# One weight load issued as two: wq by 16 and 112 partitions at the head of a decode step

## The chip, the cores and the metric

The kernel runs on one core of a Trainium2 chip. The metric is the device time of one execution in microseconds, the median of several runs. The kernel before takes 694.68 us (three runs, 694.67 to 694.69). Times inside an execution come from one profiled execution and count from the start of its span.

## What is computed

One decode step for one token of width 512. Two branches are mixed by a gate: attention with 32 query heads over 8 key/value heads and a cache of 32,768 positions, and a gated feed-forward layer of width 1,792. Everything is float32. Cut to what matters:

```python
# x (1,1,512); k_cache, v_cache (1,8,32768,128); wq (512,4096); wo (4096,512)
# w1, w3 (512,1792); w2 (1792,512); gate_w (512)
g = sigmoid((x * gate_w).sum(-1, keepdims=True))
q = (x @ wq).reshape(1, 1, 32, 128).transpose(0, 2, 1, 3)
k, v = repeat(k_cache, 4, axis=1), repeat(v_cache, 4, axis=1)
p = softmax(einsum("bhqd,bhkd->bhqk", q, k) * 128 ** -0.5)
a = einsum("bhqk,bhkd->bhqd", p, v).transpose(0, 2, 1, 3).reshape(1, 1, 4096) @ wo
b = (silu(x @ w1) * (x @ w3)) @ w2
return g * a + (1 - g) * b
```

Keys and values are 134 MB each; with the weights the kernel reads 296.23 MB from memory.

## The kernel before

The program is written out by hand: every engine has its list of instructions, and semaphores order them. Three buffers of 128 partitions by 64 KiB, `ra`, `rb` and `rc`, take all the large loads in turn. A load that fills one of them is 8 MiB, one contiguous row of 65,536 bytes for each partition.

SyncE issues all large loads (lines 115 to 149), so they form one queue. At its head stand five loads that wait for nothing: wq into all of `rc` (line 115), w1 and w3 into two parts of `rb` (116 and 117, rows of 28,672 bytes), and the first half of head 0's keys into `ra` in two parts (118 and 119). The next one, the second half of those keys into `rb` (line 121), waits until the feed-forward matmuls have read w1 and w3 from there. From then on, for each of the eight heads, two loads of keys go to `ra` and `rb` and two loads of values to `rc`, each issued when the buffer's last reader has signalled. The last head's values go to `ra` and `rb`, and wo and w2 close the queue. ScalarE issues two small loads, x and gate_w, of 2 KB each.

TensorE first turns x into columns and forms the gate's sum. Then it waits for wq (line 189) and multiplies x with it (line 194); after that it waits for w1 and w3 and does the same for the feed-forward layer (line 221). VectorE moves the query into place (206, 210), and GpSimd builds from it the windows of weights for the scores (249). Then comes a loop over heads. VectorE turns the keys in the buffer in blocks of 32 x 32 (line 335), TensorE takes the scores (line 262), the exponentials are taken on ScalarE, and one head later TensorE multiplies the probabilities with the values (line 276). At the end TensorE applies wo and w2 (lines 418 to 435).

A load's semaphore counts up by 16 when the load is complete. TensorE waits for wq with `pe.wait_ge(l_q, 16)`.

Of the kernel before, what the change touches and what calls it, by code (L numbers as in the profile page):

```python
# [9 lines left out]
P = 128  # L10
# [14 lines left out]
@with_exitstack  # L25
def kernel(ctx, tc, x, k_cache, v_cache, wq, wo, w1, w3, w2, gate_w, out):
    with tc.tile_critical():
        _program(tc.nc, x, k_cache, v_cache, wq, wo, w1, w3, w2, gate_w, out)


def _program(nc, x, k_cache, v_cache, wq, wo, w1, w3, w2, gate_w, out):
    pe, dve, act, pool, sp = nc.tensor, nc.vector, nc.scalar, nc.gpsimd, nc.sync
# [5 lines left out]
    NC = D // P  # L38
# [7 lines left out]
    def sb(name, *shape):  # L46
        return nc.alloc_sbuf_tensor(name, [P, *shape], F32).ap()

    def token(name):
        return nc.alloc_semaphore(name)  # L50
# [5 lines left out]
    ra, rb, rc = sb("ra", W), sb("rb", W), sb("rc", W)  # L56
# [34 lines left out]
    l_x, l_q, l_k0 = token("l_x"), token("l_q"), token("l_k0")  # L91
# [20 lines left out]
    kd = k_cache.rearrange("a h (p m n) d -> (a h) m p (n d)", p=P, m=2, n=NK)  # L112
    vd = v_cache.rearrange("a h (r p n) d -> (a h) r p (n d)", r=2, p=P, n=NK)
    half = W // 2
    sp.dma_start(rc, wq.rearrange("(p c) n -> p (c n)", c=NC)).then_inc(l_q, 16)
    sp.dma_start(rb[:, 0:NC * F], w1.rearrange("(p c) f -> p (c f)", c=NC)).then_inc(l_w1, 16)
    sp.dma_start(rb[:, NC * F:2 * NC * F], w3.rearrange("(p c) f -> p (c f)", c=NC)).then_inc(l_w3, 16)
    sp.dma_start(ra[:, 0:half], kd[0, 0][:, 0:half]).then_inc(l_k0, 16)
# [67 lines left out]
    dve.tensor_copy(xp[:, :, 0], mc[:, NC:2 * NC]).then_inc(t_x, 1)  # L186
    take(t_x, 2)
    n_gate = c_q.by(pe.matmul(mc[:, 0:1], ones[0:1], gsm[0:1], start=True, stop=True))
    pe.wait_ge(l_q, 16)
    for c in range(NC):  # L190
        for b in range(2):
            for j in range(4):
# [144 lines left out]
    def scaled(h):  # L337
        dve.wait_ge(c_h.sem, h + 1)
        return local.by(dve.scalar_tensor_tensor(  # L339
            otall[:, REP * h:REP * h + REP], mb[:, 0:REP], gate[:, 0:1], recip, op0=ALU.mult, op1=ALU.mult  # L340
        ))
# [57 lines left out]
    n = scaled(HKV - 1)  # L399
# [81 lines left out]
```

## Time and profile before

| what | value |
|---|---|
| median of the runs | 694.68 us |
| the profiled execution | 694.79 us |
| its span, first to last instruction | 692.5 us |
| mean granted TensorE clock | 0.783 |
| busy: TensorE, VectorE, ScalarE, GpSimd | 367.8, 309.3, 37.3, 7.1 us |
| moved from memory | 296.23 MB, 428 GB/s over the span |
| wq, from issue to landing | 21.8 us |

The profile shows one execution. In its table of slices, each digit is the busy share of a fortieth of the span in tenths. In rows of stages, the numbers are the stretch, its length, each engine's busy time with the number of its instructions, the granted clock, the mean busy share of the 16 DMA engines and what they moved in GB/s. A DMA packet is counted in the stretch in which it starts. In rows of the timeline, the numbers are start and length in microseconds, the engine (with a q for its queue, which issues loads) and line, what it writes and reads, and in brackets how long the engine idled before and what ended that.

### The profile page before, as it was taken

How to read it: one execution, taken by the hardware profiler on the slowest of the kernel's cores; microseconds unless marked ns; L12 is line 12 of the kernel's file. 1: busy time of each engine (PE TensorE's matmuls, PEld its weight loads, DVE VectorE, ACT ScalarE, POOL GpSimd, SP SyncE). 2: the span in 40 equal slices, each digit the busy share in tenths (PEclk: the TensorE clock that was granted, in tenths of full speed). 3: DMA queues.
4: the chain of work that ended last, by engine and by line, in shares of the span. 5: the costliest groups of instructions: out<-in, count | busy, mean ns of one | idle time of the engine just before them, and what ended most of it. 6: DMA issues, size and time to landing. Idle time of an engine off the chain costs nothing. (4 is left out here: it accounts for less than half of the span.)

```text
span 692.5 us, 6603 instructions
## 1 busy us (share of the span) xinstructions
PE 367.8 (53%) x2952; PEld 106.6 (15%) x2952; DVE 309.3 (45%) x208; ACT 37.3 (5%) x93; POOL 7.1 (1%) x41
## 2 busy tenths in 40 slices
PE   1626355456463734566463744466473835376475
PEld 1100011103010111103010121113010301113122
DVE  1129378191725447091816446181816356181000
ACT  0000011002000010002000010002000010001000
POOL 0000000000000000000000000000000000000000
PEclk9976598879677966778786966788677967768779
DMA  9999999999999999999999999999999999999996
GB/s 375 429 437 450 424 432 425 462 428 424 428 435 428 439 450 424 428 428 435 436 450 424 432 428 435 428 454 428 428 428 435 428 440 447 424 428 428 435 419 283
DMA packets 6069, 296.35 MB, mean 428 GB/s; under 512 B 678, under 2 KB 682, under 8 KB 940
## 3 DMA queue, kind: packets, MB, share of 16 engines
q1 hardware_dynamic: 6056, 296.23, 99.1%
q8 instruction: 6, 0.10, 0.1%
q14 instruction: 3, 0.02, 0.0%
q10 hardware_dynamic: 4, 0.00, 0.0%
HBM read 296.23 MB, written 0.00 MB: 428 GB/s over the span
## 5 line engine op out<-in xcount | busy, mean ns | idle before, releaser
L335 DVE STREAM_TRANSPOSE rb<-rb 128x2048 f32<-128x2048 f32 x64 | 141.8, 2275 | 150.9 <-DMA rb<-in_A_k_cache_dram 150.9
L335 DVE STREAM_TRANSPOSE ra<-ra 128x2048 f32<-128x2048 f32 x64 | 141.4, 2275 | 46.2 <-DMA ra<-in_A_k_cache_dram 46.2
L262 PE MATMUL psum<-rb,winbuf 128*32 128x512 f32 x512 | 91.9, 796 | 125.2 <-PEq L109 125.2
L276 PE MATMUL psum<-rc,prob 128*32 128x512 f32 x896 | 114.0, 666 | 42.7 <-PEq L109 42.7
L262 PE MATMUL psum<-ra,winbuf 128*32 128x512 f32 x512 | 82.8, 743 | 91.6 <-PEq L109 91.6
L276 PEld LDWEIGHTS psum<-rc,prob 128*32 128x32 f32 x896 | 33.7, 121 | 119.2 <-issue 119.2
L370 DVE TENSOR_REDUCE mx<-psum 128x4 f32<-128x1024 f32 x8 | 9.8, 1225 | 82.3 <-PE psum L286 82.3
L262 PEld LDWEIGHTS psum<-rb,winbuf 128*32 128x32 f32 x512 | 13.1, 120 | 201.9 <-issue 201.9
L262 PEld LDWEIGHTS psum<-ra,winbuf 128*32 128x32 f32 x512 | 14.6, 120 | 151.9 <-issue 151.9
L350 ACT COPY sbuf<-psum 128x512 f32<-128x512 f32 x16 | 9.8, 615 | 483.6 <-PE psum L262 483.6
L382 ACT ACTIVATE prob<-psum,nm 128x256 f32<-128x256 f32 x32 | 18.9, 695 | 36.5 <-DVE nm L379 36.5
L286 PE MATMUL psum<-ident,sbuf 128*64 128x64 f32 x512 | 16.7, 223 | 0.8 <-PEq L109 0.8
L286 PEld LDWEIGHTS psum<-ident,sbuf 128*64 128x64 f32 x512 | 15.6, 138 | 7.6 <-issue 7.6
L339 DVE SCALAR_TENSOR_TENSOR otall<-psum,gate,recip 128x4 f32<-128x4 f32 x8 | 1.7, 214 | 33.4 <-PE psum L296 33.4
L276 PE MATMUL psum<-rb,prob 128*32 128x512 f32 x64 | 9.1, 734 | 10.8 <-DMA rb<-in_A_v_cache_dram 10.8
L194 PE MATMUL psum<-rc,xp 128*32 128x512 f32 x64 | 9.0, 727 | 9.4 <-DMA rc<-in_A_wq_dram 9.4
L249 POOL COPY winbuf<-winraw 32x16 f32<-32x16 f32 x32 | 6.1, 191 | 537.1 <-PE psum L262 501.2
L221 PE MATMUL psum<-rb,xp 128*32 128x448 f32 x64 | 7.7, 628 | 6.4 <-DMA rb<-in_B_w_dram 6.4
L276 PE MATMUL psum<-ra,prob 128*32 128x512 f32 x64 | 8.6, 696 | 3.2 <-DMA ra<-in_A_v_cache_dram 3.2
L206 DVE STREAM_TRANSPOSE rc<-psum 128x512 f32<-128x512 f32 x2 | 1.3, 694 | 18.2 <-PE psum L194 18.2
L418 PE MATMUL psum<-rc,oq 128*32 128x512 f32 x64 | 7.3, 595 | 3.6 <-DMA rc<-in_A_wo_dram 3.3
L296 PE MATMUL psum<-fold,ob 128*128 128x4 f32 x64 | 8.4, 255 | 0.8 <-PEq L109 0.8
(60 smaller groups left out, 77.5 us busy)
## 6 DMA issues: line engine op xcount, KB each, us to landing
ra<-in_A_k_cache_dram SPq DMA_DIRECT2D x2, 4096.0 KB, 53.2
rc<-in_A_wo_dram SPq DMA_DIRECT2D x2, 4096.0 KB, 44.9
rb<-in_B_w_dram SPq DMA_DIRECT2D x2, 3584.0 KB, 34.6
ra<-in_B_w_dram SPq DMA_DIRECT2D x1, 1536.0 KB, 33.8
ra<-in_B_w_dram SPq DMA_DIRECT2D x1, 1024.0 KB, 35.9
ra<-in_B_w_dram SPq DMA_DIRECT2D x1, 768.0 KB, 37.3
ra<-in_B_w_dram SPq DMA_DIRECT2D x1, 256.0 KB, 37.4
rc<-in_A_v_cache_dram SPq DMA_DIRECT2D x14, 30.9
```

The costliest lines, as they stand in the source:

```text
L194: m = pe.matmul(pq[b][32 * j:32 * j + 32, :], xp[:, c, :], rc[:, o:o + REP * DH], start=(c == 0), stop=(c == NC - 1),)
L221: i = pe.matmul(ps[32 * j:32 * j + 32, 0:FJ], xp[:, c, :], rb[:, o:o + FJ], start=(c == 0), stop=(c == NC - 1))
L249: pool.tensor_copy(winbuf[32 * r:32 * r + 32, 16:144].rearrange("p (c k) -> p c k", k=32)[:, :, 4 * r:4 * r + REP], winraw[32 * r:32 * r + ...
L262: i = pe.matmul(s_ps[m][32 * g:32 * g + 32, :], winbuf[:, w:w + 32], region.rearrange("p (n c i) -> p c n i", c=4, i=32)[:, c, n:n + 16], ...
L276: i = pe.matmul(o_ps[32 * t:32 * t + 32, :], prob[:, w:w + 32], region[:, n * DH:(n + 4) * DH], start=(r == 0 and g == 0 and f == 0), stop ...
L286: i = pe.matmul(pf[64 * s:64 * s + 64, 64 * a:64 * a + 64], sbuf[:, a].rearrange("p i m -> p (i m)"), ident.rearrange("p (gf r s q) -> p s ...
L296: i = pe.matmul(mb[:, 0:REP], ob[:, b * P:(b + 1) * P], fold[:, 4 * b:4 * b + 4], start=(b == 0), stop=(b == 3))
L335: dve.transpose(part[:, c], part[:, c]).then_inc(t_tr, 1)
L350: act.copy(sbuf[:, :, :, m], s_ps[m].rearrange("p (n i) -> p n i", i=32)).then_inc(t_ev, 1)
L370: dve.tensor_reduce(mx, pf.rearrange("p (a q) -> p q a", q=REP), axis=AX.X, op=ALU.max).then_inc(t_mx, 1)
L382: act.activation(prob[:, 0:1024].rearrange("p (a n q) -> p n a q", a=16, q=REP)[:, :, :, q], pf.rearrange("p (n a q) -> p n a q", n=16, q= ...
L418: pe.matmul(acc[32 * t:32 * t + 32, :], oq[:, k:k + 32], rc[:, k * D:(k + 1) * D], start=(k < 4), stop=False, skip_group_check=True,)
```

## The change

The load of wq into `rc` becomes two loads that follow each other on SyncE's queue: one of partitions 0 to 15, one of partitions 16 to 127. The source rows and their places stay the same. Both add 16 to the same semaphore, and TensorE waits for 32 in place of 16. Every other instruction is the same on every engine and in the same order; the lines of the changed kernel are numbered three higher from here on.

```diff
-    sp.dma_start(rc, wq.rearrange("(p c) n -> p (c n)", c=NC)).then_inc(l_q, 16)
+
+    wqd = wq.rearrange("(p c) n -> p (c n)", c=NC)
+    sp.dma_start(rc[0:16], wqd[0:16]).then_inc(l_q, 16)
+    sp.dma_start(rc[16:P], wqd[16:P]).then_inc(l_q, 16)
...
-    pe.wait_ge(l_q, 16)
+    pe.wait_ge(l_q, 32)
```

## The prediction

> **What bounds the kernel now.** I read the page's table of slices first, then its table of DMA queues, then the chain of waits in order of time.
>
> ```profile
> span 692.5 us, 6603 instructions
> PE   1626355456463734566463744466473835376475
> DVE  1129378191725447091816446181816356181000
> DMA  9999999999999999999999999999999999999996
> q1 hardware_dynamic: 6056, 296.23, 99.1%
> ...
> 594.77 46.74 DMA ra<-in_A_v_cache_dram
> ...
> 651.05 37.27 DMA ra<-in_B_w_dram
> 688.32 0.04 issue
> 688.37 1.12 PE psum L435 x32
> ```
>
> The DMA engines are at nine tenths or more in every slice but the last, TensorE and VectorE are not. One queue, SyncE's (q1), carries all 296.23 MB and fills 99.1% of the sixteen engines' time. The chain ends on loads and 1.1 us of matmuls. So the kernel is one long line of loads. Time lost or won at its head arrives at its end, unless the line runs empty somewhere. The next view cuts the span into stages; the last three columns are the granted clock, the engines' mean busy share and GB/s.
>
> ```profile
> 0.00:21.00 21.00, 2.58 (x10) 2.43 (x10) 2.55 (x8) 1.46 (x2) 0.99 (x9) 1.00 0.96 400
> 21.00:60.00 39.00, 21.46 (x152) 4.98 (x153) 15.34 (x25) 0.54 (x1) 0.77 (x4) 0.82 1.00 429
> 60.00:200.00 140.00, 70.75 (x566) 19.07 (x570) 83.41 (x46) 9.06 (x22) 1.53 (x8) 0.77 1.00 433
> 200.00:400.00 200.00, 112.70 (x931) 32.03 (x923) 92.55 (x53) 10.17 (x25) 2.30 (x12) 0.78 1.00 435
> ```
>
> From 21 us on the line never stands: share 1.00, 429 to 435 GB/s. There is no later idle time in which a late start could be made up. The profiled execution took 694.79 us, 2.29 us more than its span; the median of three is 694.68, 0.11 us under it.
>
> **How wq comes in now.** One row of wq's load is 65,536 B, one partition's share. A packet is counted in the stretch in which it starts, with its whole time and bytes, so a share can be above 1.
>
> ```profile
> 1.80:1.90 0.10, 0.00 (x0) 0.00 (x0) 0.10 (x1) 0.10 (x1) 0.10 (x2) 1.00 0.07 20
> 1.90:2.00 0.10, 0.00 (x0) 0.00 (x0) 0.10 (x1) 0.10 (x1) 0.09 (x1) 1.00 3.90 1311
> ...
> 1.00:2.00 1.00, 0.00 (x0) 0.00 (x0) 0.57 (x3) 0.28 (x1) 0.74 (x5) 1.00 0.40 133
> 2.00:3.00 1.00, 0.00 (x0) 0.00 (x0) 0.30 (x2) 1.00 (x1) 0.00 (x0) 1.00 2.77 918
> ...
> 19.00:20.00 1.00, 0.00 (x0) 0.00 (x0) 0.00 (x0) 0.00 (x0) 0.00 (x0) 1.00 2.42 1049
> rc<-in_A_wq_dram SPq DMA_DIRECT2D x1, 21.8
> ```
>
> The stretch from 19 to 20 us holds one round: 1.049 MB, sixteen rows, 2.42 us for each engine, so 27.1 GB/s an engine. The first round (rows 1.00 and 2.00) holds 133 + 918 KB, again sixteen rows and the 2 KB of x, and takes 0.40 + 2.77 = 3.17 us a row. It begins at 1.9 us; the small load of x begins at 1.8. Eight rounds are 7 x 2.42 + 3.17 = 20.1 us, which with the start near 2 us and the landing agrees with 0.96 + 21.8 = 22.8.
>
> **What the change does to that, part by part.**
>
> *SyncE.* One issue more, ahead of five that stand in a row:
>
> ```profile
> 0.91 0.52 ACTq L152 DMA_DIRECT2D ob<-in_A_x_dram  x1
> 0.96 0.39 SPq L115 DMA_DIRECT2D rc<-in_A_wq_dram  x1
> 1.41 0.41 SPq L116 DMA_DIRECT2D rb<-in_B_w_dram  x1
> 1.86 0.43 SPq L117 DMA_DIRECT2D rb<-in_B_w_dram  x1
> 2.34 0.53 SPq L118 DMA_DIRECT2D ra<-in_A_k_cache_dram  x1
> 2.91 0.44 SPq L119 DMA_DIRECT2D ra<-in_A_k_cache_dram  x1
> ```
>
> From issue to issue is 0.45 to 0.57 us, so w1, w3 and the two key halves are issued about half a microsecond later. They are hidden: w1's rows have their turn behind the rows of wq, at about 22 us, and it would be issued at 1.9. The second part of wq would be issued at about 1.4 and, at the 1.0 us from issue to first packet shown above, be ready at 2.4, before any row of the first part is through (1.9 + 2.42 = 4.3). If that cover were gone, half a microsecond would be lost. The sixteen additional completions cost nothing I can see: the stretch 21 to 60 us crosses several load boundaries at share 1.00; its 429 against 433 GB/s is 0.9% of 39 us, under 0.4 us for all of them.
>
> *The start.* The most the short first load can win is the 3.17 - 2.42 = 0.75 us by which the first round is long, and 0.1 to 0.2 us by which x's packet starts sooner: 1.0 us in all, if filling the queue with 128 rows is what holds the first round back. The least is nothing. I take -0.5.
>
> *The first part, 16 partitions.* This is the disputed price: no load of before covers part of the partitions with large rows. What the trace shows is that sixteen engines with 128 partitions between them, eight each, keep 27.1 GB/s all the time, as sixteen separate ways into the memory would allow. Sixteen neighbouring partitions need not have sixteen ways. If a way serves partitions dealt out singly, all sixteen are open: 2.42 us, nothing lost. If it serves one block of eight, two are open: 16 / 2 x 2.42 = 19.4 us, +16.9. If it serves two blocks of four, four are open: 4 x 2.42 = 9.7 us, +7.3. I take the last: it lies nearest the geometric middle of the two ends (6.8 us) together with eight ways (4.8 us), and of these two I choose the dearer because the old load already had every way open and can only lose. By the Trainium skill, SBUF — State Buffer, section "Door 1: The DMA port swizzle", four neighbouring partitions share a port, so that 0 to 15 reach four of sixteen ports, and 1 MiB to them was measured there at 104 GB/s; as an estimate from that page this part would take 10.1 us, and the term would be +7.7. No run here shows it yet.
>
> *The second part, 112 partitions.* Seven rows an engine. With every way open, 7 x 2.42 = 16.9 us. Two bounds with the four-way layout: four ways have given up four rows each, the other twelve still have eight to take, so at the least 8 x 2.42 = 19.4, +2.4. If each engine has seven neighbouring rows, the sixteen engines write seven partitions apart, and in a given round some ways meet two of them and others none; were each round as long as its worst way, 7 x 4.84 = 33.9, +16.9. I take +8.0, a little under the middle (9.7), because the engines are not in step: their first packets start over some 0.7 us. A load dealt out like the old one, each engine on a way of its own, would stand at the low end.
>
> *What waits.* TensorE's wait for wq only counts to 32 now. Behind it stand the query's matmuls, w1, w3 and then everything else on TensorE:
>
> ```profile
> 22.83 9.03 PE L194 MATMUL psum<-rc,xp 128*32 128x512 f32 x64 [9.45 <-DMA rc<-in_A_wq_dram]
> 31.69 3.18 PE L221 MATMUL psum<-rb,xp 128*32 128x448 f32 x32
> 41.28 4.48 PE L221 MATMUL psum<-rb,xp 128*32 128x448 f32 x32 [6.41 <-DMA rb<-in_B_w_dram]
> 45.83 0.33 SPq L121 DMA_DIRECT2D rb<-in_A_k_cache_dram  x1
> 60.69 8.89 DVE L335 STREAM_TRANSPOSE ra<-ra 128x2048 f32<-128x2048 f32 x4 [0.82 <-DMA ra<-in_A_k_cache_dram]
> ```
>
> TensorE idles 6.41 us before w3, so the query is not the limit; and SyncE's next load (L121) is issued at 45.83 while the key half is still landing until 60.69, a cover of 14.9 us. All these loads stand behind wq in one line and shift with it, so the cover shifts too, and neither adds to the sum.
>
> *Sum.* 0 (SyncE) - 0.5 (start) + 7.3 (first part) + 8.0 (second part) = +14.8 us. On 694.79 that is 709.6; on the median, 709.5.
>
> **The rivals.**
>
> *Not slower.* Every row keeps 2.42 us, either because neighbouring partitions do not share a way, or because engines are tied to partitions, so that the first part just queues rows on a few engines and the second gives those fewer: then the change doesn't do what it says, and the work per engine is the old one. The gain is at the most the 1.0 us of the start: 693.7 to 694.8. For it: every bulk load in the trace holds 429 to 435 GB/s whatever the row's size. Against it: all of them address 128 partitions. It decides if the first sixteen rows are through by about 5 us. The Trainium skill, DMA: Bandwidth & Descriptors, section "Why a DMA increments its semaphore by 16 and not by 1", speaks against the tied version: the number of engines is the largest up to 16 that divides the rows, which gives all sixteen for 16 and for 112.
>
> *Only the first part pays.* The second is dealt so that it stands at its low end: -0.5 + 7.3 + 2.4 = +9.2, 703.9. The steady share of 1.00 for 128 rows speaks for a good dealing; an uneven seven speaks against it.
>
> *Both parts pay in full.* Row by row in turn, sixteen neighbours in every round of the second part: 7 x 7.3 more, +58 in all, 752. Nothing in the profile excludes it, but a deal that makes this of 112 rows would have made it of 128, whose rounds take 2.42 us.
>
> **How the numbers follow.** Forecast 0.44, only the first part 0.22, both in full 0.07, not slower 0.27. Of the last, 0.21 is within 0.2% (1.4 us, about what a measurement of this kernel can tell from no change) and 0.06 is a gain above the bound that I worked out for the start. So slower 0.73, same 0.21, faster 0.06. The forecast's own range is 704 to 714, from second-part terms of +2.4 to about +13. The range for 8 in 10 also takes in the first-part rival and the unchanged case: 694.0 to 714.0. The 752 is left out.
>
> **What would show it.** In the profile of after: the first sixteen rows' share, 3.17 now, near 9.7; wq landing near 38 us in place of 22.8; the wait before the query longer by about 15 us and w1, w3 and the first key turns later by as much; the stages from 60 us on unchanged at 1.00 and 433 GB/s, and the same 37 us of loads at the end. A first round of 2.4 to 3.2 us with a landing at 22 to 23 makes the forecast wrong; a first round of 9.7 with a landing near 32 makes the second term wrong; a rate below 430 GB/s after 60 us would mean that the engines stay out of step, which I price at nothing.

## The result, and the profile after

The changed kernel takes 714.8 us (median of five runs, 714.75 to 716.24) against 694.67 us for the one before (694.58 to 694.69): 20.1 us more by the medians. Over all the runs the ratio is 1.0295, with a 95% interval of 1.0283 to 1.0306. The profiled execution of after is the run of 716.24 us, the longest of the five, and its span is 21.6 us longer than that of before. The page of after, the lines that answer to those of before, and the row of GB/s in each fortieth of the span:

```profile
span 714.1 us, 6604 instructions
DMA  9999999999999999999999999999999999999996
GB/s 176 235 335 431 454 423 449 419 430 444 422 444 433 422 448 426 430 444 422 445 430 426 441 430 430 444 426 441 430 426 448 422 437 433 430 444 422 431 425 254
q1 hardware_dynamic: 6072, 296.23, 98.9%
```

The DMA engines look as busy as before, because an engine that is held up in a packet counts as busy. The row of GB/s tells more: 176, 235 and 335 in the first three slices, and from the fourth on 419 to 454 up to the last, as in the kernel before (419 to 462 between its first slice and its last). Nearly the whole loss lies in the first 54 us. The later stages are as they were:

```profile
60.00:200.00 140.00, 73.48 (x560) 19.08 (x560) 77.62 (x45) 9.07 (x22) 1.53 (x8) 0.77 1.01 436
200.00:400.00 200.00, 110.07 (x820) 29.46 (x820) 98.95 (x56) 8.97 (x23) 1.53 (x8) 0.73 1.00 432
```

So is the end of the chain of waits (start, length, what): 37 us of loads and 1.1 us of matmuls.

```profile
672.49 37.40 DMA ra<-in_B_w_dram
709.89 0.04 issue
709.93 1.12 PE psum L438 x32
```

Here is the head of after, cut at the starts of the rounds of sixteen rows of wq. In each stretch sixteen rows of 65,536 B start (GB/s times length is 1.05 MB in all of them), so share times length is the mean time of one row.

```profile
1.90:9.90 8.00, 0.00 (x0) 0.00 (x0) 0.40 (x2) 1.10 (x1) 0.09 (x1) 1.00 1.06 131
9.90:15.70 5.80, 2.57 (x10) 2.43 (x10) 1.64 (x4) 0.17 (x1) 0.00 (x0) 1.00 0.93 181
15.70:20.40 4.70, 0.00 (x0) 0.00 (x0) 0.04 (x1) 0.00 (x0) 0.00 (x0) 1.00 1.00 223
20.40:23.70 3.30, 0.00 (x0) 0.00 (x0) 0.00 (x0) 0.00 (x0) 0.00 (x0) 1.00 1.01 318
23.70:27.50 3.80, 0.00 (x0) 0.00 (x0) 0.00 (x0) 0.00 (x0) 0.00 (x0) 1.00 1.02 276
27.50:31.70 4.20, 0.00 (x0) 0.00 (x0) 0.00 (x0) 0.00 (x0) 0.00 (x0) 1.00 1.07 250
31.70:36.30 4.60, 0.00 (x0) 0.00 (x0) 0.00 (x0) 0.00 (x0) 0.00 (x0) 1.00 1.01 228
36.30:40.80 4.50, 0.00 (x0) 0.00 (x0) 0.00 (x0) 0.00 (x0) 0.00 (x0) 1.00 1.02 233
```

The first part, one round, has a mean row of 1.06 x 8.00 = 8.5 us, where the first round of before had 3.17. The second part takes from 9.9 to 40.8, 30.9 us for seven rounds that would take 16.9 at 2.42 us. Two of its rounds, the third and the fourth, are quicker than the others (3.3 and 3.9 us a row against 4.5 to 5.4). The single packets of the trace show more. In its second round the sixteen rows start over 0.9 us (15.77 to 16.64), and every one of them takes 4.7 to 4.9 us. In the third, two rows take 4.8 us and the other fourteen 2.9 to 3.4.

Behind that, everything shifts together; these are rows of after's timeline:

```profile
44.85 8.68 PE L197 MATMUL psum<-rc,xp 128*32 128x512 f32 x64 [29.51 <-DMA rc<-in_A_wq_dram]
53.37 3.21 PE L224 MATMUL psum<-rb,xp 128*32 128x448 f32 x32
61.87 4.84 PE L224 MATMUL psum<-rb,xp 128*32 128x448 f32 x32 [5.29 <-DMA rb<-in_B_w_dram]
66.78 0.33 SPq L124 DMA_DIRECT2D rb<-in_A_k_cache_dram  x1
81.25 4.50 DVE L338 STREAM_TRANSPOSE ra<-ra 128x2048 f32<-128x2048 f32 x2 [0.81 <-DMA ra<-in_A_k_cache_dram]
```

The query starts 22.0 us later than before, w3's matmuls 20.6, SyncE's next load 21.0 and the second key half 20.6. TensorE still idles before w3 (5.29 us), so the loads and not the matmuls set the pace there.

### The profile page after: what moved, and what is told of

Read it like the earlier page. It is cut to its first block, busy times and chain, and to the rows that moved or that the text cites. A ratio compares the mean times of both kernels' runs of the same rounds, so it can differ in the third digit from the quotient of the medians.

```text
span 714.1 us, 6604 instructions
## 1 busy us (share of the span) xinstructions
PE 374.0 (52%) x2952; PEld 106.8 (15%) x2952; DVE 309.3 (43%) x208; ACT 37.3 (5%) x93; POOL 7.1 (1%) x41
## 5 line engine op out<-in xcount | busy, mean ns | idle before, releaser
L265 PE MATMUL psum<-rb,winbuf 128*32 128x512 f32 x512 | 93.7, 811 | 125.2 <-PEq L109 125.2
L265 PE MATMUL psum<-ra,winbuf 128*32 128x512 f32 x512 | 87.3, 780 | 85.4 <-PEq L109 85.4
L265 PEld LDWEIGHTS psum<-ra,winbuf 128*32 128x32 f32 x512 | 14.8, 122 | 150.7 <-issue 150.7
```

The lines of the kernel that those rows point to most:

```text
L265: i = pe.matmul(s_ps[m][32 * g:32 * g + 32, :], winbuf[:, w:w + 32], region.rearrange("p (n c i) -> p c n i", c=4, i=32)[:, c, n:n + 16], ...
```

## The experiments

A way stands for a path by which engines write into partitions; engines that write over the same one share its rate. Theory A: sixteen engines reach few neighbouring partitions over few ways, and each part of wq loses by the ways that its rows share. Rivals: the cut as such, or the short load at the head, costs (C); neighbouring rows collide on the side of the memory that is read (B); only the odd count of seven rows an engine costs (D). Each time below is a median, with that of the kernel before from the same chip beside it. The code is cut to the lines that matter; `wqd` is the view of wq that the change made.

**The same cut along columns.** All 128 partitions in both loads.

```diff
-    sp.dma_start(rc, wq.rearrange("(p c) n -> p (c n)", c=NC)).then_inc(l_q, 16)
+    wqd = wq.rearrange("(p c) n -> p (c n)", c=NC)
+    sp.dma_start(rc[:, 0:2048], wqd[:, 0:2048]).then_inc(l_q, 16)
+    sp.dma_start(rc[:, 2048:W], wqd[:, 2048:W]).then_inc(l_q, 16)
...
-    pe.wait_ge(l_q, 16)
+    pe.wait_ge(l_q, 32)
```

> wq still comes as two loads of 1 and 7 MiB, but cut along the columns, each over all 128 partitions. Theory A (16 engines writing into few neighbouring partitions share ways; the layout of the rows costs, the second load as such costs nothing): no loss, 693.7 to 694.8 us, rounds of 16 full rows keep 27 GB/s an engine, wq lands at 22 to 23 us. Rival C (cutting a load in two, or a short load at the head, costs by itself): slower by several us, up to the 20 us of the change.

Measured: 694.34 us against 694.62, ratio 0.9996 (0.9987 to 1.0005). As many loads, bytes and completions as in the change, and nothing is lost: C falls. In the profile the query starts at 22.55 us in place of 22.83, and the medians differ by 0.3 us too; but the ratio's interval takes in 1, so a gain from the short load at the head is not shown.

```profile
22.55 8.61 PE L196 MATMUL psum<-rc,xp 128*32 128x512 f32 x64 [14.30 <-DMA rc<-in_A_wq_dram]
```

**Each part alone.** The kernel before, with one more load ahead of wq into `ra`, which is free until the keys come; the keys' first load waits for it on a new semaphore. Of the two added loads below, each kernel has one.

```diff
+    sp.dma_start(ra[0:16], wqd[0:16]).then_inc(l_e, 16)
+    sp.dma_start(ra[16:P], wqd[16:P]).then_inc(l_e, 16)
     sp.dma_start(rc, wq.rearrange("(p c) n -> p (c n)", c=NC)).then_inc(l_q, 16)
...
+    sp.wait_ge(l_e, 16)
     sp.dma_start(ra[:, 0:half], kd[0, 0][:, 0:half]).then_inc(l_k0, 16)
```

> The kernel before with one more load at the head: wq's rows 0 to 15 once more, into partitions 0 to 15 of ra, which is free until the keys come. It prices the first part alone. Theory A: 16 rows over few ways take about 8.5 us each as in the changed kernel, wq starts near 10.9 us and runs at full rate: +8.1, 702.8 us. If 16 rows were as fast as a round of the full load: +2.4, 697.1 us.

> The kernel before with one more load at the head: wq's rows 16 to 127 into partitions 16 to 127 of ra. It prices the second part alone. Theory A with the rounds seen in the changed kernel (30.9 us for seven): about +30.7, 725.4 us. If the second part was slow only because the first had put the engines out of step, seven rounds at 2.42 us: +16.9, 711.6 us.

Measured: 704.21 and 725.33 us against 694.62, so +9.6 and +30.7. At 2.42 us a round the two would cost 2.4 and 16.9; the excess is 7.2 us for the 16 rows and 13.8 us for the 112. The second part is slow by itself, without the first ahead of it.

The 16 rows alone came out 1.4 us above the 702.8 that was expected. The round behind them holds what was left out:

```profile
1.90:9.60 7.70, 0.00 (x0) 0.00 (x0) 0.39 (x2) 1.09 (x1) 0.09 (x1) 1.00 1.11 136
9.60:14.40 4.80, 1.41 (x6) 1.41 (x7) 1.35 (x2) 0.00 (x0) 0.00 (x0) 1.00 0.81 219
14.40:16.80 2.40, 1.16 (x5) 1.02 (x5) 0.32 (x2) 0.17 (x1) 0.00 (x0) 1.00 1.01 437
```

The sixteen rows take 8.5 us each, and the first round of the full wq behind them 3.9 in place of 2.42; the next is at full rate.

The rounds with 112 rows alone at the head, and then two rounds of the full wq behind them:

```profile
1.90:6.20 4.30, 0.00 (x0) 0.00 (x0) 0.40 (x2) 1.09 (x1) 0.09 (x1) 1.00 1.12 244
6.20:10.80 4.60, 0.00 (x0) 0.00 (x0) 0.00 (x0) 0.00 (x0) 0.00 (x0) 1.00 1.01 228
10.80:14.40 3.60, 2.02 (x8) 1.94 (x8) 1.35 (x2) 0.00 (x0) 0.00 (x0) 1.00 0.97 291
14.40:17.60 3.20, 0.55 (x2) 0.50 (x2) 0.32 (x2) 0.17 (x1) 0.00 (x0) 1.00 1.06 328
17.60:21.70 4.10, 0.00 (x0) 0.00 (x0) 0.00 (x0) 0.00 (x0) 0.00 (x0) 1.00 1.07 256
21.70:26.10 4.40, 0.00 (x0) 0.00 (x0) 0.00 (x0) 0.00 (x0) 0.00 (x0) 1.00 1.02 238
26.10:30.60 4.50, 0.00 (x0) 0.00 (x0) 0.00 (x0) 0.00 (x0) 0.00 (x0) 1.00 1.02 233
30.60:34.30 3.70, 0.00 (x0) 0.00 (x0) 0.00 (x0) 0.00 (x0) 0.00 (x0) 1.00 0.85 283
34.30:36.70 2.40, 0.00 (x0) 0.00 (x0) 0.00 (x0) 0.00 (x0) 0.00 (x0) 1.00 1.01 437
```

The third and fourth rounds are the quick ones again, each with two rows of 4.3 to 4.8 us among rows of 3.1 to 3.7. Behind the 112 rows, the first round of 128 partitions has a mean row of 3.1 us and the second runs at 437 GB/s.

**Halves.** `rc[0:64]` and `rc[64:P]` in place of 16 and 112.

> wq as two loads of 64 partitions. Theory A (four neighbouring partitions share a way, and the second 32 of 64 share them with the first 32, so 64 partitions open 8 of 16 ways): every round takes 4.84 us in place of 2.42, 38.7 us for wq, +19.4, 714.0 us. Rival D (only uneven counts such as 7 rows an engine, or very few rows, are slow): 64 rows are 4 an engine, no loss, 694.7 us.

Measured: 715.98 us against 694.62, +21.4. D falls: four rows an engine, an even count, cost as much as the change. A round in the middle takes 5.12 us a row by its packets; the expected 4.84 was 0.28 us a round too low.

```profile
11.70:16.80 5.10, 2.57 (x10) 2.43 (x10) 1.68 (x4) 0.17 (x1) 0.00 (x0) 1.00 1.00 206
```

**Which side.** wq as eight loads of 16 rows in place of the one load, with neighbouring or spread rows on either side; TensorE waits for 128. The loop has one of the three lines below: neighbours on both sides, then spread rows that are read, then spread partitions that are written. In the second and third kernel rows of wq are exchanged, so that the query is that of another matrix.

```diff
+    for j in range(8):
+        sp.dma_start(rc[16 * j:16 * j + 16], wqd[16 * j:16 * j + 16]).then_inc(l_q, 16)
+        sp.dma_start(rc[16 * j:16 * j + 16], wqd[j:P:8]).then_inc(l_q, 16)
+        sp.dma_start(rc[j:P:8], wqd[16 * j:16 * j + 16]).then_inc(l_q, 16)
```

> wq as eight loads of 16 rows, each from 16 neighbouring rows of the source into 16 neighbouring partitions: the change's first part eight times over. Theory A (ways on the side of the buffer): every round takes 9.0 to 9.7 us, wq about 75 us in place of 20, 745 to 753 us. Theory B (neighbouring rows collide on the side of the memory that is read): the same. It sets the scale for the next two.

> Eight loads of 16 rows into 16 neighbouring partitions, but from source rows eight apart, so rows of wq are exchanged and q is that of another matrix. Theory A: as slow as with neighbouring source rows, 745 to 753 us. Theory B: the source rows are spread and the loss is gone or far smaller, 695 to 716 us.

> Eight loads of 16 rows into partitions eight apart, from 16 neighbouring source rows, rows of wq exchanged as before. Theory A: partitions eight apart open 8 of 16 ways, two engines on each, 5.12 us a round as in the load by halves, 41 us for wq, about 715.5 us. Theory B: 745 to 753 us.

Measured: 750.0, 749.08 and 716.0 us against 694.73. One round in the middle of wq, with neighbours on both sides:

```profile
28.10:37.40 9.30, 0.00 (x0) 0.00 (x0) 0.00 (x0) 0.00 (x0) 0.00 (x0) 1.00 1.00 113
```

The same with spread rows that are read:

```profile
18.90:28.20 9.30, 0.00 (x0) 0.00 (x0) 0.00 (x0) 0.00 (x0) 0.00 (x0) 1.00 1.00 113
```

And with spread partitions that are written:

```profile
6.60:11.70 5.10, 2.58 (x10) 2.43 (x10) 1.52 (x3) 0.05 (x1) 0.00 (x0) 1.00 1.01 206
```

Spreading the rows that are read changes nothing (9.3 us and 9.3 us); spreading the partitions that are written halves the round (5.1 us). B falls: the loss is on the side of the buffer. Sixteen neighbouring partitions move 113 GB/s; 64 neighbours, or sixteen partitions eight apart, move 206.

**The deal of the 112 rows.** The second part once more at the head of the kernel before, dealt by hand in seven loads of 16 rows, seven partitions apart.

```diff
+    for r in range(7):
+        sp.dma_start(ra[16 + r:P:7], wqd[16 + r:P:7]).then_inc(l_e, 16)
```

> The kernel before with rows 16 to 127 once more into ra at its head, as the second part alone, but dealt by hand: seven loads of 16 rows whose partitions are seven apart, so that in each an engine has the row that it has if the deal gives each engine seven neighbours. If that is the deal and any way with two engines holds all engines up: the same as the one load of 112, +30.7, 725.3 us, with rounds near 4.6 us and the third and fourth shorter. If only the engines that meet are held up: +24 to +26, 719 to 721 us, most packets at 2.4 us. If the deal is another: packet times of another pattern.

Measured: 725.61 us against 694.73, +30.9, as the single load of 112 (+30.7), and round for round nearly the same rates (the third and fourth differ by 8 and 3%):

```profile
1.90:6.30 4.40, 0.00 (x0) 0.00 (x0) 0.40 (x2) 1.08 (x1) 0.09 (x1) 1.00 1.01 238
6.30:10.90 4.60, 2.39 (x10) 2.34 (x10) 1.52 (x3) 0.00 (x0) 0.00 (x0) 1.00 1.03 228
10.90:14.80 3.90, 0.18 (x1) 0.10 (x1) 0.15 (x1) 0.17 (x1) 0.00 (x0) 1.00 0.93 269
14.80:17.90 3.10, 0.00 (x0) 0.00 (x0) 0.00 (x0) 0.00 (x0) 0.00 (x0) 1.00 1.08 338
17.90:22.00 4.10, 0.00 (x0) 0.00 (x0) 0.00 (x0) 0.00 (x0) 0.00 (x0) 1.00 1.08 256
22.00:26.40 4.40, 0.00 (x0) 0.00 (x0) 0.00 (x0) 0.00 (x0) 0.00 (x0) 1.00 1.06 238
26.40:31.00 4.60, 0.00 (x0) 0.00 (x0) 0.00 (x0) 0.00 (x0) 0.00 (x0) 1.00 0.99 228
```

So a load of 112 rows behaves as if each engine had seven neighbouring partitions. The trace does not name the engine of a packet, so the deal itself is inferred. Count the ways with the layout that the halves and the spread loads bear out, four neighbours to a way and partitions 32 apart on the same one: in the third and fourth rounds one way gets two engines, in the five others two ways do. The quick rounds are those with one, and the two slow rows in them fit the pair.

**Who waits for a shared way.** The first kernel has both loads below, into `ra`: one with one shared way behind wq, and one with two behind w1. The second has the latter alone, directly behind wq.

```diff
+    sp.dma_start(ra[18:P:7], wqd[18:P:7]).then_inc(l_e, 16)
+    sp.dma_start(ra[16:16 + 106:7], wqd[16:16 + 106:7]).then_inc(l_e, 16)
```

> Two loads of 16 rows more, into ra, each alone between loads of 128 rows: behind wq one of partitions 18, 25, .. 123 (by the layout of the ways only one way gets two engines: two of the sixteen engines meet), behind w1 one of partitions 16, 23, .. 121 (two ways get two engines: four engines meet). Theory A1 (an engine that waits for a shared way holds the others up): behind wq the pair takes 4.8 to 5.1 us and the other fourteen about 3.1, behind w1 all sixteen about 4.6; together +8 to +10 us, 703 to 705 us. Theory A2 (only those that meet wait): 2.42 us for fourteen and for twelve of the sixteen; the slowest engine is behind by at most 5 to 10 us.

> One load of 16 rows more, partitions 16, 23, .. 121 of ra, directly behind wq, where all engines are in step: by the layout of the ways two ways get two engines each, four engines meet, twelve have a way of their own. In the run before, the single pair took 5.1 to 5.2 us and the fourteen others 2.63 to 2.77; the two pairs came behind w1, with the engines still apart, and nearly all took 4.3 to 4.9. Theory A1 (two shared ways hold all engines up): all sixteen near 4.6 us here too. Theory A2 (only those that meet wait, the rest was a leftover of the engines being apart): four at 5.1, twelve at 2.6 to 2.8. Time: 699.5 to 700.5 us in both, since the slowest engine is behind by 5 us.

Measured: 707.84 us (706.86 to 708.81) against 694.64, and 699.68 against 694.58. The first came out 3 to 5 us above what was expected of it: behind w1 the engines were still apart from the load before, and single rows took up to 6.8 us. What the theories differ in is seen directly behind wq, where the engines are nearly in step (the sixteen rows start within 0.6 us in both). The stretch in which those sixteen rows start, in the kernel with one shared way there:

```profile
21.50:24.00 2.50, 0.96 (x8) 0.31 (x12) 0.00 (x0) 0.00 (x0) 0.00 (x0) 1.00 1.19 419
```

The same stretch in the kernel with two:

```profile
21.50:24.00 2.50, 0.69 (x4) 0.20 (x8) 0.00 (x0) 0.00 (x0) 0.00 (x0) 1.00 1.72 419
```

Means of 2.97 and 4.29 us a row. The sixteen packet times of each in the trace, in us:

```
one shared way:  2.63 2.63 2.63 2.63 2.64 2.65 2.65 2.65 2.65 2.66 2.66 2.66 2.66 2.77 5.11 5.20
two shared ways: 3.95 4.11 4.12 4.19 4.20 4.21 4.24 4.25 4.29 4.34 4.34 4.42 4.45 4.45 4.54 4.56
```

With one shared way the pair takes 5.1 to 5.2 us and the others 2.63 to 2.77, between the 3.1 of theory A1 (an engine that waits holds the others up) and the 2.42 of theory A2 (only those that meet wait). With two, all sixteen are slow, though by the layout twelve of them have a way of their own: A2 falls, and A1 holds with 4.0 to 4.6 us where it expected about 4.6. Why one shared way nearly spares the others and two don't was not tried further and stays open.

**The order of the two loads, and a shorter first cut.** 112 rows first, then 16; and the cut along columns at 512 in place of 2048.

> The change with its two loads in the other order, 112 rows first. If the two prices simply add: 714.8 us, within 1 us. If the first load's loss is a matter of the start of the queue, or the second's a matter of engines put out of step by the first: less, toward 704 to 708 us.

> The cut along columns with a shorter first load: 128 partitions by 512 columns (256 KiB), then the rest. What a short first load wins at the start is bounded by 1.0 us: 693.7 to 694.7 us. If it is the number of descriptors of the first load (128 in both) that holds the first round back, the same as the cut at 2048 columns, 694.3 us.

Measured: 716.29 us against 694.64, +21.6, 0.5 us outside what adding allowed and on the far side from less. The order makes 1.5 us, so the two prices don't come from the place at the head. The shorter cut takes 694.55 against 694.64 (ratio 0.9999, 0.9990 to 1.0008). Its median is 0.1 us lower, that of the longer cut 0.3; neither can be told from no change by its interval. No version here is shown to beat the kernel before.

## Why the prediction was right or wrong

- **The bound, and that a delay at the head arrives at the end:** right. 432 to 436 GB/s from 60 to 650 us in both, and of the 20.6 us by which the second key half is late none is made up: the end of that run comes 21.6 us later, and the medians differ by 20.1. ("From 21 us on" was a little too wide: in the last 40 us of before, where the queue ends, the share is 0.91.)
- **SyncE's additional issue and the sixteen completions, 0:** right. The cut along columns has both and loses nothing.
- **The start, -0.5:** not shown. The cut along columns, with a short first load over all partitions, reads -0.3 (694.62 to 694.34), which its interval can't tell from nothing.
- **The first part, +7.3 from four ways:** right. Alone it costs 7.2 us above a full-rate round, part of it in the round behind, and in the steady case sixteen neighbours take 9.3 us where four ways gave 9.7. The prediction took four ways as the dearer of two near the middle of its bounds, and that this hit was luck as far as the trace of before goes; the runs since show it. The Trainium skill, SBUF — State Buffer, "Door 1: The DMA port swizzle", agrees: 104 GB/s to 16 partitions and 196 to 64 are measured there, 113 and 206 here, and partitions 32 apart share a port there, as the halves show here.
- **The second part, +8.0:** this step failed. It measured +13.8 alone, near the upper bound that the prediction worked out, +16.9, from each round being as long as its worst way. The step took a value "a little under the middle (9.7), because the engines are not in step". Being out of step did not help: in the change the second round's rows start over 0.9 us and all take 4.7 to 4.9, and behind wq two shared ways slow the twelve engines that by the layout share nothing. The two rounds with one shared way are 2.8 us shorter than 2 x 4.84, most of the distance from 16.9 to 13.8; the five others are 1.3 us under 5 x 4.84 together, and the round behind them is 0.7 us over 2.42.
- **The sum:** 7.2 + 13.8 = 21.0 from the separate runs, 20.1 in the change itself; 14.8 was forecast. The 5.8 us by which the second part was sized too low are more than the whole miss of 5.3. The time lies 0.8 us above the range, whose upper end came from a second part of at most about 13 (with 13 the sum gives 714.5; 714.0 stands for 12.5).
- **What waits on TensorE:** right; the cover moved with the line, and the wait before the query grew from 9.45 to 29.51 us.
- **The rivals:** "not slower" and its version with engines tied to partitions are out: in the change the sixteen rows of the first part start within 1.2 us of each other (1.99 to 3.21), so they do not queue one behind another, and each takes 7.8 to 9.3 us. "Only the first part" is out by the 112 rows alone, "both in full" by their rounds of 3.2 to 4.6 us; its price (+58 on 694.68 gives 752.7) is near what sixteen neighbours in every round do cost, 750.0 us.

## What to carry to other kernels

In a kernel bound by loads, cut a large load along its rows' contents and not along its partitions: every piece should still reach all 128 partitions. Where a piece must be of fewer partitions, work out which engines write to the same ways in each round. Where two ways or more are shared, price the round near its worst way, not by the mean over the engines: 4.4 to 5.4 us here against a worst way of 5.12. A round with one shared way cost less, 3.3 to 3.9 us. DMA engines that read as busy may be held up: look at GB/s beside the share.

## What the runs showed of the hardware that was not expected

In one round behind wq, two shared ways slow all sixteen engines (3.95 to 4.56 us a row in place of 2.42), while one slows the other fourteen by about a tenth (2.63 to 2.77). Two engines on a way take 5.12 us a row, more than twice 2.42, or 25.6 GB/s for the way; four take 9.3 us, less than four times, 28 GB/s. And a load of 112 partitions behaves as if dealt in blocks of seven neighbours, while 128 partitions keep 2.42 us a row, as without a shared way.
